# New ranks for a planned instruction order, one unit's sums moved to DMA, and a small copy moved to ScalarE

## The chip, the cores and the metric

The kernel runs on one core of a Trainium2 chip. The metric is the device time in microseconds; of several runs the median is taken. Lower is better.

## The reference, cut to what matters

Inputs are q, k, v and x of 2048 x 640 in bfloat16 (the reference passes q where the second block has its x), small filters, and weights of an MLP.

```python
# block A: a gated long convolution
k_shift = sum(k_pad[:, t:t + S, :] * shift_k[:, ks - 1 - t] for t in range(4))
kv = k_shift * v
y = irfft(rfft(kv, padded to 2S) * rfft(ssm_k, padded to 2S))[:S] + kv * ssm_D
a = q * y
# block B: a shifting MLP and a second MLP
h = gelu(layernorm(x) @ w1)
hs = concat(h quarters shifted by +1, -1, +2, -2 in the sequence) @ w2
x1 = x + hs
b = x1 + gelu(layernorm(x1) @ w3) @ w4
# both, gated
g = sigmoid((x * gate_w).sum(-1))
out = g * a + (1 - g) * b
```

## The kernel before

**One list, five queues.** The kernel does not write its instructions into the engines' queues directly. Each is put down as a node of a program `P` with its engine, what it reads and writes, an estimated cost and a tag; `P.stage` is appended to the tag, so that "mm1:2" is the first matmul of row group 2. `P.schedule` then makes the order: it keeps a clock of its own for TensorE, ScalarE, VectorE, GpSimd (POOL) and SyncE (SP), and picks again and again the node that can start earliest, and among equals the one of the highest rank. Ranks stand in the table `P.PRIO` by tag. The loads from HBM go through a model link of a given rate, so the clock also assumes when data arrives. The result is a fixed order for each engine; at run time each engine works through its queue in that order and waits on semaphores where needed. A node whose inputs come later on the chip than on the planner's clock holds up all that stands behind it in its queue.

**Storage.** All tiles lie in one SBUF tensor, "arena", so the profile calls nearly everything arena. PSUM is used as four pairs of banks.

**Block B.** Rows of x are laid out as 8 row groups (rho) of 2 x 128 partitions. Layer norm 1 takes its statistics by VectorE (`ln_bn`, bn_stats at L686, tags bn and ln) for rows 0 and 2 to 7, and by ScalarE sums (tags sum and sq, L496) for row 1. The reciprocal root is one POOL instruction (L661), then come a small product on VectorE (L662) and the normalised rows (L705, tag xn). TensorE transposes them (L718, tag xTp), ScalarE evicts them (xTe, by the helper at L511). `mm1` (L794) multiplies by w1: three jobs for each of four row pairs, the third with a small rearranged copy of w1, `w1t`, made by one copy of 128 x 640 (L565). The gelu evictions write HT. The shifts of the last quarter-columns are small POOL DMAs (L822, tag tail). Zeros at HT's edges are memsets (L779 for the pads, L784), and HT's first part holds the row of shift taps at the very start, so the pads wait for the four small matmuls that spread these taps over the partitions (L589, tag shk). The gate's sums are 80 one-column matmuls (L752). `mm2` (L840, and L843 for the residual) has four groups of four jobs, tags mm2:4 to mm2:7, then layer norm 2, `mm3` (L883, w3 in two halves; the second half lies where w2 was and is loaded after the last mm2) and `mm4` (L902), whose evictions are added to x by accumulating POOL DMAs (tag addB). mm3's results lie in 20 slots where HT was; one stage of mm3 fills 12.

**Block A.** VectorE forms k_shift * v (tags kv and kve, by the helper `tt` at L484; for the second half of the rows, two of the sums are accumulating POOL DMAs, kva). TensorE transposes the filter (L641, tag tap). Four units, one for each half of the channels and each half of the frequencies (0,0), (0,1), (1,0), (1,1), stages 0 to 3, are done as: forward transforms of filter and signal (L938, tags fwdh and fwdk), window and butterflies (win, bh, bk), a pointwise complex product (pw), and a fold. Units named in `PW_DMA` use `pointwise_dma`, which leaves two of the sums to accumulating POOL DMAs (L522, tags pwa with 320 KB and pwb with 640 KB); the others use `pointwise`, all on VectorE. After the units of a half, `inverse` (L1099) makes eight jobs; its evictions are scaled by the gate (gy), multiplied by q and added to x (fin; for half 0 the addition is a DMA, addy), and rows go out by SP.

**Loads.** All of x, w1, w2, k with its halo, v, the transform table FM and the filter (ssm) are loads on SP's queue without inputs, so their order is their rank. POOL loads w3, w4 and the table GM later.

Nodes of one tag share one rank in the kernel before:

```python
for n in self.nodes:
    n.prio = self.PRIO.get(n.tag, n.prio)
```

Of the kernel before, what the change touches and what calls it, by code (L numbers as in the profile page):

```python
# [10 lines left out]
ACTF = mybir.ActivationFunctionType  # L11
# [68 lines left out]
class Prog:  # L80
# [66 lines left out]

    def schedule(self):

        for n in self.nodes:  # L150
            n.base = frozenset(n.deps)
            for d in n.deps:
                d.users.append(n)
        for n in reversed(self.nodes):
            tail = max((u.prio for u in n.users), default=0.0)
            n.prio = tail + (n.cost if n.kind == "c" else n.cost + 2.0 + n.bytes / self.RATE)
        for n in self.nodes:
            n.prio = self.PRIO.get(n.tag, n.prio)
        self._forward()

    def _forward(self):
# [10 lines left out]
        known_at = {}  # L172
        pair_free = [0.0] * PAIRS
        pair_job = [None] * PAIRS
        link = 1.6
        xlink = 0.0

        def move(at, nbytes):
# [20 lines left out]
        while left:  # L199
# [16 lines left out]
            n = best[1]  # L216
            e = n.eng
# [6 lines left out]
            elif n.kind == "dma" and e == "pool" and n.bytes < self.SMALL:  # L224
                link = move(link, n.bytes)
                n.end = t + 4.5
            elif n.kind == "dma":
                link = move(max(link, t), n.bytes)
# [132 lines left out]
def bass_gated_mix__ssm_conv_h3__mixer_s_mlp__prompt_kernel(  # L361
# [9 lines left out]
    PW_NEG = ()  # L371
    BF_DMA = ()
    INV_SPLIT = ((1, 0), (1, 4))
    PW_DMA = ((0, 0), (0, 1), (1, 0))
    LN1_ROWS = ((0,), (1,), (2, 3), (4, 5), (6, 7))
    LN1_DVE, LN2_DVE = ((0,), (2, 3), (4, 5), (6, 7)), (0, 1)
    P = Prog(nc)
# [51 lines left out]
    w1t = V(oW12 + 3200, 640).rearrange("p (c f) -> p c f", c=5)  # L429
# [4 lines left out]
    GM = V(oGM, 4096).rearrange("p (a i r s k) -> p a i r s k", a=2, i=2, r=4, s=2)  # L434
# [9 lines left out]
    ident = V(oID, 128)  # L444
# [35 lines left out]
    def dve(fn, r, w, n, psum=False, tag="", **kw):  # L480
        return P.op("dve", lambda e, ps: fn(e), r=r, w=w, cost=c_dve(n, psum), tag=tag, **kw)
# [4 lines left out]
    def act(o, i, func, n, scale=None, bias=None, acc=None, tag="", group=None, job=None, accgroup=None):  # L486
        r = [x for x in (i, scale, bias) if x is not None and not isinstance(x, float)]
        kw = {}
        if scale is not None:
            kw["scale"] = scale  # L490
        if bias is not None:
            kw["bias"] = bias
        if acc is not None:
            kw["accum_out"] = acc
        naps = sum(1 for x in (scale, bias) if x is not None and not isinstance(x, float))
        node = P.op("act", lambda e, ps: e.activation(o, i, func, **kw), r=r, w=[o], cost=c_act(n, naps, acc is not None),  # L496
                    tag=tag, group=group)
        if acc is not None:
            P._track(node, [], [acc], accgroup)
        return node  # L500
# [58 lines left out]
    for c in range(2):  # L559
# [2 lines left out]
    load_halo(0)  # L562
    load_k(0, 0)
    w1s, w1d = w1v.rearrange("p c (g f) -> p c g f", g=4)[:, :, :, 128:160], w1t.rearrange("p c (g f) -> p c g f", g=4)
    P.op("pool", lambda e, ps: e.tensor_copy(w1d, w1s), r=[w1s], w=[w1d], cost=1.2, tag="w1t")  # L565
    load_k(0, 1)
    load_x("sp", 0, 4, 8)
    load_x("sp", 1, 4, 8)
# [3 lines left out]
          w=[GWT], nbytes=100000, after=[late], tag="gw")  # L572
# [184 lines left out]
    v0, r0, nm0 = [stat(0, f)[:, :, 0:2] for f in ("var", "rs", "nm")]  # L757
# [18 lines left out]
    SHIFT = [1, -1, 2, -2]  # L776
    for col in (0, 257):
        z = HT[:, 0:4, :, col:col + 1]
        dve(lambda e, z=z: e.memset(z, 0.0), [], [z], 32, group="pad")  # L779
    for j, d0 in enumerate(SHIFT):  # L780
        rs = slice(0, d0) if d0 > 0 else slice(8 + d0, 8)
        col = 1 if d0 > 0 else 256
        z = HT[32 * j:32 * j + 32, 4, rs, col:col + 1]
        dve(lambda e, z=z: e.memset(z, 0.0), [], [z], 2, group="tail")  # L784
    RAW = [V(oGM + 512 * i, 512) for i in range(2)]
    for sc in range(4):
        P.stage = sc
        for fp in range(3):
# [13 lines left out]
            else:  # L802
                raw = RAW[sc % 2]
                evict(job, raw, lambda ps: bank(ps, 0, 512), ACTF.Gelu_apprx_tanh, 512, tag="gelu1t")
                for j, d0 in enumerate(SHIFT):
# [4 lines left out]
                    for carry, lst in todo.items():  # L810
                        k0, rho0, n = lst[0][0], lst[0][1], len(lst)
# [8 lines left out]
                        else:  # L820
                            i = i.rearrange("p (r q) -> p r q", r=n)
# [265 lines left out]
    def inverse(half, slot0, slot1):  # L1087
# [50 lines left out]
    inverse(1, "s3", "k0")  # L1138

    P.PRIO = {  # L1140
# [25 lines left out]
    }  # L1166
    P.schedule()
    P.assign_waits()
# [30 lines left out]
```

## Time and profile before

| | us |
|---|---|
| median of 3 runs | 244.91 (243.86 to 245.47) |
| the profiled execution | 245.85 |
| its span | 244.1 |
| TensorE busy | 223.6 |
| VectorE busy | 215.7 |
| ScalarE busy | 154.3 |
| POOL busy | 57.9 |

The profile is of one execution. Its span runs from the first to the last instruction shown; the time has 1.75 us more around it. Busy times are sums of instruction lengths; issuing a DMA counts for none of the engines except where POOL makes it. In rows of the chain, a start and a length in us are followed by an engine or "issue" and a line of the kernel; in rows of the timeline, the number in brackets is the idle time before and what ended it.

### The profile page before, as it was taken

The page shows a single profiled execution, that of the slowest core. Times are in us where ns is not written, and L with a number is a line of the kernel's source. Part 1 is how long each engine was busy: PE and PEld are TensorE (multiplying, and loading weights), DVE is VectorE, ACT ScalarE, POOL GpSimd, SP SyncE. Part 2 cuts the span into 40 slices and gives each one's busy share as a digit, 9 for nine tenths or more (in the row PEclk, how much of TensorE's full clock was granted, in tenths as well). Part 3 has the DMA queues.
Part 4 walks back from the last instruction along what each step waited for, and adds up shares of the span by engine and source line. Part 5 has one row for each costly group of instructions (what it writes and reads, how often), then busy time and mean ns, then how long its engine had stood idle before and what let it go on. Part 6 is the DMA issues. An engine that isn't in the chain of part 4 may idle for free.

```text
span 244.1 us, 3961 instructions
## 1 busy us (share of the span) xinstructions
PE 223.6 (92%) x1557; PEld 142.4 (58%) x1569; DVE 215.7 (88%) x337; ACT 154.3 (63%) x236; POOL 57.9 (24%) x70
## 2 busy tenths in 40 slices
PE   0579999999999999969999999999999998999990
PEld 0236576577777775525677645577546773777760
DVE  4899989996999758998989699799994899999992
ACT  5536899647468999956997456652257224127881
POOL 5311452451013040145002121001220011015910
PEclk9999999979999999999999999999999999999997
DMA  6999998098019649665585325403248034934998
GB/s 217 369 398 331 397 362 301 22 246 156 3 19 191 88 113 293 141 129 107 106 104 183 56 51 77 85 3 54 53 56 110 0 55 70 382 88 74 160 214 253
DMA packets 29938, 37.32 MB, mean 153 GB/s; under 512 B 12464, under 2 KB 22960, under 8 KB 29792
## 3 DMA queue, kind: packets, MB, share of 16 engines
q0 software_dynamic: 9424, 15.21, 32.0%
q1 hardware_dynamic: 20496, 21.86, 29.7%
q8 instruction: 12, 0.20, 0.3%
q14 instruction: 6, 0.05, 0.1%
HBM read 21.79 MB, written 2.62 MB: 100 GB/s over the span
## 4 chain that ended last, share of the span: by engine, by line
PE 88%; DMA 5%; DVE 3%; ACT 1%; issue 1%; SPq 0%; ACTq 0%
PE PS L902 21%; PE PS L883 18%; PE PS L938 14%; PE PS L794 10%; PE PS L840 9%; PE PS L1099 7%; DMA arena<-in_B_w_dram 3%; PE PS L641 3%; PE PS L718 2%; PE PS L843 2%; DMA arena<-in_A_q_dram 1%; DVE arena L686 1%; ACT arena L511 1%; PE PS L752 1%; DVE arena L705 1%
## 5 line engine op out<-in xcount | busy, mean ns | idle before, releaser
L484 DVE TENSOR_TENSOR arena<-arena 128x1280 bf16<-128x1280 bf16 (+2 forms) x192 | 180.3, 999 | 12.3 <-ACT arena L511 9.9
L511 ACT ACTIVATE arena<-PS 128x640 bf16<-128x640 f32 (+3 forms) x129 | 96.6, 821 | 42.5 <-PE PS L883 21.9
L522 POOL DMA_DIRECT2D arena<-arena x26 | 29.4, 1207 | 106.3 <-ACT arena L511 64.8
L883 PE MATMUL PS<-arena 128*128 128x512 bf16 x232 | 51.9, 379 | 2.4 <-DMA arena<-in_B_w_dram 2.0
L902 PE MATMUL PS<-arena 128*128 128x320 bf16 x384 | 52.8, 299 | 1.1 <-ACT arena L511 1.1
L511 ACT ACTIVATE arena<-PS,arena 128x320 bf16<-128x320 f32 (+1 forms) x48 | 27.6, 615 | 36.9 <-PE PS L902 34.2
L902 PEld LDWEIGHTS PS<-arena 128*128 128x128 bf16 x384 | 37.5, 98 | 16.1 <-ACT arena L511 1.6
L883 PEld LDWEIGHTS PS<-arena 128*128 128x128 bf16 x240 | 23.3, 98 | 29.6 <-DMA arena<-in_B_w_dram 2.5
L938 PE MATMUL PS<-arena 128*128 128x320 bf16 x256 | 36.4, 299 | 0.0
L938 PEld LDWEIGHTS PS<-arena 128*128 128x128 bf16 x256 | 25.1, 98 | 10.6
L840 PE MATMUL PS<-arena 128*128 128x320 bf16 x160 | 27.6, 310 | 0.0
L794 PE MATMUL PS<-arena 128*128 128x512 bf16 x96 | 23.8, 404 | 1.6 <-ACT arena L511 1.4
L686 DVE BATCH_NORM_STATS2 arena<-arena 128x6 f32<-128x320 bf16 x44 | 19.0, 467 | 4.9 <-DMA arena<-in_A_q_dram 2.5
L496 ACT ACTIVATE arena<-arena 128x640 bf16<-128x640 bf16 (+2 forms) x30 | 21.8, 756 | 1.7 <-DMA arena<-in_A_q_dram 1.7
L840 PEld LDWEIGHTS PS<-arena 128*128 128x128 bf16 x160 | 16.1, 101 | 6.8
L794 PEld LDWEIGHTS PS<-arena 128*128 128x128 bf16 x100 | 10.0, 103 | 13.6 <-issue 4.4
L1099 PE MATMUL PS<-arena 128*128 128x320 bf16 x128 | 17.6, 299 | 0.0
L1099 PEld LDWEIGHTS PS<-arena 128*128 128x128 bf16 x128 | 12.5, 98 | 4.9
L661 POOL TENSOR_TENSOR arena<-arena 128x4 f32<-128x4 f32 (+1 forms) x9 | 10.1, 1118 | 16.7 <-DVE arena L691 11.4
L705 DVE TENSOR_SCALAR arena<-arena 128x640 bf16<-128x640 bf16 x32 | 12.4, 440 | 1.3 <-issue 1.2
L822 POOL DMA_DIRECT2D arena<-arena x18 | 9.7, 544 | 8.5 <-ACT arena L511 8.5
L645 ACT ACTIVATE arena<-PS 128x1280 bf16<-128x1280 bf16 x8 | 9.5, 1263 | 2.4 <-PE PS L641 2.4
(43 smaller groups left out, 73.3 us busy)
## 6 DMA issues: line engine op xcount, KB each, us to landing
arena<-arena POOLq DMA_DIRECT2D x7, 640.0 KB, 5.6
arena<-in_A_q_dram SPq DMA_DIRECT2D x6, 640.0 KB, 8.0
arena<-in_B_w_dram POOLq DMA_DIRECT2D x4, 960.0 KB, 7.7
arena<-arena POOLq DMA_DIRECT2D x11, 320.0 KB, 3.7
arena<-in_A_ssm_k_dram SPq DMA_DIRECT2D x5, 512.0 KB, 11.4
arena<-in_A_k_dram SPq DMA_DIRECT2D x4, 640.0 KB, 17.1
arena<-in_A_v_dram SPq DMA_DIRECT2D x4, 640.0 KB, 20.5
out_dram<-arena SPq DMA_DIRECT2D x16, 160.0 KB, 2.1
```

Of the source, the lines that this page charges most:

```text
L484: return dve(lambda e: e.tensor_tensor(o, a, b, op), [a, b], [o], n, tag=tag, **kw)
L496: node = P.op("act", lambda e, ps: e.activation(o, i, func, **kw), r=r, w=[o], cost=c_act(n, naps, acc is not None), tag=tag, group=group)
L511: node = P.op("act", lambda e, ps: e.activation(ov, inner(ps), func, **kw), r=r, w=[o], cost=c_act(n, len(r), acc is not None), job=job, t ...
L522: P.dma("pool", lambda e, ps: e.dma_start(o, i, accum_op=ALU.add, max_dma_last_dim=2560), r=[o, i], w=[o], nbytes=3 * 256 * n, cost=1.2, t ...
L686: dve(lambda e, o=o, x=x: e.bn_stats(o, x), [x], [o], 640, tag="bn", group=("bn", l, rho, c))
L705: P.op("dve", lambda e, ps, b=b, x=x, rs=rs, nb=nb: e.tensor_scalar(b, x, rs, nb, op0=ALU.mult, op1=ALU.add), r=[x, rs, nb], w=[b], cost=0 ...
L794: fns.append(lambda e, ps, b=b, c=c, lhsT=lhsT, sc=sc: e.matmul(bank(ps, b, 512), lhsT, XT[:, c, 2 * sc:2 * sc + 2, :], start=(c == 0), st ...
L840: fns.append(lambda e, ps, hh=hh, ft=ft, lhsT=lhsT, last=by_dma and ft == 4: e.matmul(bank(ps, hh, 320), lhsT, w2v[:, ft, 320 * hh:320 * h ...
L883: fns.append(lambda e, ps, b=b, ft=ft, c=c, sc=sc: e.matmul(bank(ps, b, 512), w3v[ft // 6][:, c, 128 * (ft % 6):128 * (ft % 6) + 128], XT[ ...
L902: fns.append(lambda e, ps, hh=hh, ft=ft, lhsT=lhsT: e.matmul(bank(ps, hh, 320), lhsT, w4v[:, ft, 320 * hh:320 * hh + 320], start=(ft == 0) ...
L938: fns.append(lambda e, ps, r=r, ri=ri, s=s, b=b, rhs=rhs: e.matmul(bank(ps, b, 320), FM[:, kap, r, s, ri, :], rhs, start=(s == 0), stop=(s ...
L1099: fns.append(lambda e, ps, kap=kap, ri=ri, c=c, r=r, s=s: e.matmul(bank(ps, c, 320), GM[:, kap, ri, r, s, :], Qs[kap][:, r, ri, c, :], sta ...
```

## The change

- `PW_DMA` gets (1, 1), so the last unit, too, leaves two sums to POOL DMAs.
- w1's small copy moves from POOL to ScalarE.
- The pads get a tag of their own, with ranks.
- In the planner's clock the link starts at 0.8 in place of 1.6.
- Nodes of one tag are split into up to four parts, in their order of writing, with a rank each: "mm1:2.0" is the first quarter of mm1's stage 2. All ranks are new. Where a tag has one node only, it keeps its name.

```diff
-        for n in self.nodes:
-            n.prio = self.PRIO.get(n.tag, n.prio)
+        parts = {}
+        for n in self.nodes:
+            parts.setdefault(n.tag, []).append(n)
+        for tag, ns in parts.items():
+            for i, n in enumerate(ns):
+                if len(ns) > 1:
+                    n.tag = f"{tag}.{i * min(len(ns), 4) // len(ns)}"
+                n.prio = self.PRIO.get(n.tag, self.PRIO.get(tag, n.prio))
...
-        link = 1.6
+        link = 0.8
...
-    PW_DMA = ((0, 0), (0, 1), (1, 0))
+    PW_DMA = ((0, 0), (0, 1), (1, 0), (1, 1))
...
-    P.op("pool", lambda e, ps: e.tensor_copy(w1d, w1s), r=[w1s], w=[w1d], cost=1.2, tag="w1t")
+    act(w1d, w1s, ACTF.Copy, 640, tag="w1t")
...
-        dve(lambda e, z=z: e.memset(z, 0.0), [], [z], 32, group="pad")
+        dve(lambda e, z=z: e.memset(z, 0.0), [], [z], 32, group="pad", tag="pad")
...
-        dve(lambda e, z=z: e.memset(z, 0.0), [], [z], 2, group="tail")
+        dve(lambda e, z=z: e.memset(z, 0.0), [], [z], 2, group="tail", tag="pad")
```

Ranks that the prediction speaks of, before and after (quarters 0 to 3 where there are several):

```
                 before   after
shk (the load)   151      247
x0, x1, x2       180 186 158   217, 212, 186 183
w1               147      182
x4               126      178
w2               96       119 146 95 39
k1               26       47 148
ln:0             103      140 60 235 74
bn:2             11       228 144 101 248
xn:0, xn:1       33, 97   230 198, 50 86
mm1:0            77       64 57 59
mm1:2            47       113 295 201
mm2:5            32       190 271 217 259
mm2:6            10       195 156 184 249
mm2:7            104      183 159 190 158
gate             54       181 179 68 97
tap:1            114      154 291 248 136
fwdh:1           59       223 219 160 12
fwdk:1           25       148 206 213 241
fwdk:2           86       45 124 288 103
mm4:2            30       21 11 4 32
addB:3           3        207 193
pwb:3            (none)   22
```

112 rows, old and new, of the table final are left out of this document.

## The prediction

> **What bounds the kernel now.** First the page's busy times and its slices, then the chain of work that ended last, in order of time, then what each engine did around the places where that chain is not matmuls.
>
> ```profile
> span 244.1 us, 3961 instructions
> PE 223.6 (92%) x1557; PEld 142.4 (58%) x1569; DVE 215.7 (88%) x337; ACT 154.3 (63%) x236; POOL 57.9 (24%) x70
> PE   0579999999999999969999999999999998999990
> DVE  4899989996999758998989699799994899999992
> PEclk9999999979999999999999999999999999999997
> ```
>
> TensorE is full from the third slice to the last but one; VectorE is nearly as full. Both matter: whoever moves one must keep the other fed. The chain, with its few places that are not plain matmul time:
>
> ```profile
> 9.78 0.15 DVE arena L705
> 12.41 1.24 PE PS L718 x10
> 13.67 1.25 ACT arena L511
> 15.05 6.45 PE PS L794 x20
> ...
> 50.41 1.33 PE PS L840 x5
> ...
> 58.64 0.68 PE PS L840 x5
> ...
> 99.94 8.15 DMA arena<-in_B_w_dram
> 108.14 5.79 PE PS L883 x26
> ...
> 220.15 17.40 PE PS L1099 x128
> ```
>
> Columns are start, length, what. Dense TensorE work begins at 15.05 (mm1, L794) and ends at 220.15 + 17.40 = 237.55; 6.6 us of last eviction, products and output follow. In these 222.5 us TensorE is short of four things. Two are idle time: 2.03 us before 108.14, while the second half of w3 arrives, and 1.11 us at 206.94 (mm4 of the last stage behind a gelu eviction). Two are slow matmuls: the first 20 of L794 take 6.45 us where 19 later ones take 4.26 (about 2.0 us lost), and after the gate's one-column matmuls five L840 take 1.33 instead of 0.68, twice, and one L843 0.27 instead of 0.14: 1.4 us lost. The rest of the time can only go by another start, another end, or new holes.
>
> The w3 hole, and the start of the kernel on VectorE and GpSimd (start, length, engine):
>
> ```profile
> 99.47 6.64 PE L883 MATMUL PS<-arena 128*128 128x512 bf16 x29
> 108.14 6.65 PE L883 MATMUL PS<-arena 128*128 128x512 bf16 x29 [2.03 <-DMA arena<-in_B_w_dram]
> ```
>
> ```profile
> 9.84 0.22 DVE L779 MEMSET arena<- 128x32 bf16 x2
> 10.13 0.43 DVE L705 TENSOR_SCALAR arena<-arena 128x640 bf16<-128x640 bf16 x1
> 10.42 0.72 POOL L565 COPY arena<-arena 128x640 bf16<-128x640 bf16 x1 [1.61 <-DMA arena<-in_B_w_dram]
> 10.49 0.67 DVE L662 TENSOR_TENSOR arena<-arena 128x2 f32<-128x2 f32 x1
> ```
>
> The load of w3's second half is issued at 99.94, when the last mm2 matmul (L843) has ended, and takes 8.15 us; 29 mm3 matmuls cover 6.64 of them. At the start, the pads and a small product stretched beside GpSimd's copy (0.67 us; the nine L662 have a median of 0.16) lie between row 0's and row 1's normalised halves, which the first transposes await.
>
> **The change, part by part.** All sums are against the profiled execution's own 245.85 us (span 244.1 and 1.75 around it); the median of the three runs is 244.91, 0.94 below, and the same difference is then taken from it.
>
> *Pads and w1's copy.* The two memsets cost 0.15 of VectorE time on the chain (9.98 to 10.13 less the issue), the copy some 0.5 (0.67 less 0.16). The copy becomes one 640-element ScalarE activation: 0.75 us by the row of L496 (792 ns mean). ScalarE sits idle 1.49 us before the first transposes' eviction and 4.47 before the first gelu, so it costs nothing; without that cover, 0.75.
>
> *Shift taps' row first.* One more SP issue of 0.33 us lies ahead of x0. Its matmuls (2.42 us from 7.24) and four evictions (2.49 us from 8.00) go some 4 us earlier, into time in which TensorE and ScalarE mostly idle; but on ScalarE they now stand ahead of row 1's four sums (3.93 to 6.92 before), which then end near 8.6.
>
> *Ranks, at the start.* With the new table row 0's mean sign (ln:0.1, 60) and its normalise wait behind statistics of rows 2 and 3 (bn:2, 101 to 248), and row 1's normalise has 50 and 86. From the end of row 0's statistics (6.85) I lay out eight statistics of 0.41 and four aggregates of 0.12, 3.8 us; four normalised halves, 1.6; small products 0.8; pads 0.15: row 1 is ready at 13.2 instead of 12.27, +0.9. In return rows 2 and 3 are ready early: 20 transposes (1.12 us at 21.50) move into idle time before mm1, and take part of its slow stretch, half of 1.1, with them: -1.1 -0.5. If the 1.14 us that VectorE stood with nothing shown before 9.78 are not repeated, it is earlier by that; if they come on top, later. Start and slow stretch together: -0.7 by these rows; I take -0.5, ends -1.8 and +2.0.
>
> *Ranks, in the middle.* All mm2 jobs now have 156 or more, above much of the forward transforms (fwdh:1.3 has 12, fwdk:1.0 148, fwdk:2.0 45); before, mm2:6 had 10 and came last. mm2 is 16 jobs of 1.63 us, 26.1; from 50.41, with three forward transforms of 4.35 between, it ends near 50.4 + 26.1 + 13.1 + 1.4 = 91, not 99.65. The w3 load then lands near 100, and behind mm2 there are 6.6 us of mm3 on the first half and at least one transform of 4.35, together more than 8.15. So the 2.03 us go: -2.0, ends 0 and -2.0. It rests on the load not standing in POOL's in-order queue behind an accumulate that waits for VectorE. The hole of 1.11 at 206.94 stays: mm3's last jobs reuse activation slots that mm4:2 reads, and mm4:2 has the lowest ranks (4 to 32), so the same order closes the stage. Ends 0 and -1.1, value 0.
>
> *Ranks, the gate.* gate.0 is at 181, above the last transposes of the taps (tap:1.0 154, tap:1.3 136); before, gate and taps lay back to back for 3.1 us (47.30 to 50.41), and the clock fell. If only the gate's 2.3 us lie together the 1.4 us may partly go. Value -0.5, ends 0 and -1.4.
>
> *Last unit's sums.* Two VectorE sums go: one of 1280 (0.82) and one of 2560 (1.49), 2.3 us. Two accumulates come on POOL's queue, 1.2 us each to issue, 3.7 us (320 KB) and 5.6 us (640 KB) to land. After the larger is issued VectorE still has 1.49 + 0.82 + 1.49 + 0.82 of products and 1.6 of folds that don't read its result, 6.2 against about 5.6 to 6.8: covered. The fold's last operations ended near 233, where the inverse's fifth job of half 1 (220.15 + 8.7 + 4.35 = 233.2) needs them. So the 2.3 us bring nothing to TensorE by themselves, but let its end come up to 2.3 us earlier without waiting. Value 0, ends 0 and +5 (below).
>
> *Queue order of the loads.* The same bytes, other order: w2's last quarter (39) and k's third block (47) are last, where w2 was issued at 4.78. Value 0, ends 0 and +3.
>
> Sum: -0.5 -2.0 -0.5 = -3.0: 242.85 for a run like the profiled one, **241.9** for the median.
>
> **The rivals.**
> *Gains spent again (about 244.9).* The start comes +2.0 and the w3 hole closes by as much: 0. For it: VectorE is 88% busy and its list is served in a fixed order, so an early hole closed is a later one opened (it already stood 3.67 us before the last unit). Against it: TensorE has 50 us of mm4 to fill with.
> *Loads late (247.4), the other side.* TensorE's queue is in order. Before, the loads ended with the seventh slice (301 GB/s, then 22), about 43 us, and mm1 ended at 47.3. mm2:5 has 217 to 271 in three of its quarters, above mm1:2.0 (113) and mm1:0 (57 to 64), so mm2 may stand near 40 in the queue; w2's last quarter then holds everything behind it for 3 us, and VectorE's third shift unit waits for k as long. 244.9 + 3.0 less the 0.5 of the start. It decides once mm2 stands ahead of about 43 us. Against it: mm2 also needs all of mm1 for most rows.
> *The last sum behind POOL's queue (about 247).* POOL waited 11.27 us for the addB at 214.76 and 5.67 for the one at 221.28. If the large accumulate (rank 22, addB:3 193 and 207) stands behind the second, it lands near 228, eight folds of 0.75 follow, and the inverse waits about 5 us: 241.9 + 5.
> *The slow matmuls.* The rows show slow matmuls after time with little TensorE work, and none later. If the 1.4 us after the gate go wholly: 241.9 - 0.9 = 241.0; if a further such stretch comes, 243.3. The Trainium skill (TensorE: Matmul & The Clock Gate, "The HAM clock gate") says that the clock is halved by default and released after some 3.4 us of sustained work, in windows that run freely. The trace agrees in the granted clock of 0.50 from 50 to 53 us; by that rule alone the place of the gate among the mm1 jobs settles this rival.
>
> **How the numbers follow.** Forecast 0.42 (own range 240.2 to 243.8); gains spent again 0.20; loads late 0.18; last sum late 0.08; slow matmuls otherwise 0.12. About 1%, 2.45 us, is what a measurement of this kernel can tell from no change. Faster by more: two thirds of the forecast, most of the last rival, a little of the second: 0.44. Slower by more: the two late cases and a part of the spent one: 0.26. Within: 0.30. The range runs from 238.6 (start -1.8, w3 -2.0, gate -1.4, and the 1.1 hole) to 248.0 (loads late, above).
>
> **What would show it.** Right: the first L794 between 14.5 and 16, transposes of rows 2 and 3 before it; no DMA piece of in_B_w_dram in the chain and the last L843 before 93; VectorE's last fold at or before 231; the first L1099 near 217. Wrong: TensorE idle near 40 to 45 with a load as its releaser, L1099 waiting for L484, an L522 behind ScalarE in front of the last folds, or VectorE idle for more than the 16 us that its waits from 59 to 223 us add up to now.

## The result, and the profile after

| | before | after |
|---|---|---|
| median, us | 244.38 (243.79 to 245.47) | 246.91 (246.15 to 247.69) |
| the profiled execution | 245.85 | 246.95 |
| its span | 244.1 | 245.2 |
| TensorE busy / VectorE busy | 223.6 / 215.7 | 223.4 / 214.1 |

The ratio after to before is 1.0142, 95% interval 1.0095 to 1.0188, from four runs of each: the change makes the kernel 1.4% slower, where 1.2% faster was forecast (241.9 to 244.91). All lines behind the planner's stand 7 lines further down in the kernel after (mm1 is L801, mm2 L847 and L850, mm3 L890, mm4 L909, the forward transforms L945, the inverse L1106, VectorE's `tt` L491, the eviction helper L518, POOL's accumulates L529, loads L525, the DMA transposes L719).

The page of after, busy times and slices (share of the span in brackets; tenths in forty slices):

```profile
span 245.2 us, 3981 instructions
PE 223.4 (91%) x1569; PEld 141.9 (58%) x1569; DVE 214.1 (87%) x335; ACT 155.6 (63%) x237; POOL 62.1 (25%) x71
PE   3099999899999999959999999999999998999990
DVE  4979999799995979989949999999994999973992
PEclk9999999999999999979999999999999999999999
```

TensorE's row is as full as before but for the ends and one dip; the granted clock falls in the 18th slice, near 107 us; the drop of the clock near 50 us, in the ninth slice of before, is gone. TensorE's timeline in after, from the first transposes on, only rows with idle time in front of them (start, length, line, shapes, count, idle time and its releaser):

```profile
12.55 4.00 PE L725 MATMUL PS<-arena 128*128 128x128 bf16 x40 [7.54 <-DVE arena L698]
48.08 1.26 PE L945 MATMUL PS<-arena 128*128 128x320 bf16 x8 [0.73 <-DVE arena L771]
51.13 0.84 PE L847 MATMUL PS<-arena 128*128 128x320 bf16 x5 [0.16 <-ACT arena L652]
107.67 6.11 PE L890 MATMUL PS<-arena 128*128 128x512 bf16 x20 [3.03 <-DMA arena<-arena]
208.09 13.21 PE L909 MATMUL PS<-arena 128*128 128x320 bf16 x96 [1.12 <-ACT arena L518]
```

At its first mm3 matmul, 93.68, all mm2 and 128 transform matmuls are done. Before has done as much, and 20 mm3 matmuls (4.32 us) besides, at 99.65, so its equal mark is 95.33: after is 1.65 ahead. At the first mm4 it is behind, 125.52 to 124.39, with equal work done (100 mm3 and 168 transform matmuls against 90 and 184, 10 x 0.216 for 16 x 0.136). So 2.8 us go between the two marks, although before has its own hole of 2.03 there. The chain of waits shows the place (start, length, what):

```profile
95.94 0.37 DVE arena L712
96.31 0.02 issue
96.33 11.09 DMA arena<-arena
107.42 0.25 issue
107.67 6.11 PE PS L890 x20
...
221.31 7.61 PE PS L1106 x56
...
228.93 9.97 PE PS L1106 x72
```

Layer norm 2 of a row group is done at 96.31, its DMA transpose (tag xT) is issued at 96.33 and lands 11.09 us later. (The inverse then begins at 221.3, not near 217, and TensorE ends at 238.9 instead of 237.55.) What stands ahead of it is on POOL's timeline, and what is usual for a transpose in the answer for L719 (us to landing, least, median, most):

```profile
93.48 2.64 POOL L525 DMA_DIRECT2D arena<-in_B_w_dram  x3 [4.25 <-DMA arena<-arena]
```

```profile
DMA to landing us min/median/max: 2.6/2.7/11.1
```

Three loads of 960 KB, w3's second half and both halves of w4, go out in one 2.64 us piece just before the transpose. In before the longest landing of a transpose was 6.3, and the same loads lay far apart:

```profile
87.72 1.75 POOL L518 DMA_DIRECT2D arena<-in_B_w_dram  x2 [8.46 <-DMA arena<-arena]
99.94 0.92 POOL L518 DMA_DIRECT2D arena<-in_B_w_dram  x1 [9.41 <-PE PS L843]
```

The kernel makes all three wait for the DMA transposes of rows 0 and 1 (`after=turned[4]`), w3's half also for the last mm2. In before, w4's two left when these transposes had landed, at 87.72, and w3's half 12 us later, behind mm2. In after the transposes land later, at 93.48, and mm2 has ended by then (near 91); w3's half is first in POOL's queue, w4's two are next, and all three leave together. The windows of after then show the second price, the granted clock behind the hole (window, its length, PE busy, and further on PEclk, DMA share, GB/s):

```profile
100.00:107.00 7.00, 4.63 (x22) 1.96 (x20) 7.00 (x10) 6.65 (x13) 1.39 (x2) 1.00 1.20 263
107.00:109.00 2.00, 1.33 (x4) 0.53 (x5) 2.00 (x3) 0.00 (x0) 2.00 (x2) 0.65 0.97 140
109.00:111.00 2.00, 2.00 (x6) 0.63 (x5) 1.06 (x4) 0.00 (x0) 1.65 (x2) 0.50 1.07 193
111.00:113.60 2.60, 2.60 (x13) 1.18 (x12) 2.57 (x7) 1.94 (x2) 1.01 (x1) 1.00 0.77 144
```

The 20 matmuls take 6.11 us instead of the 4.32 of the next such group in the chain: 1.8 lost on top of 3.03 (together 4.8).

The start (VectorE, ScalarE) answers the lines shown of before:

```profile
6.62 0.09 DVE L786 MEMSET arena<- 128x32 bf16 x1
11.61 0.80 DVE L712 TENSOR_SCALAR arena<-arena 128x640 bf16<-128x640 bf16 x2
12.39 0.80 DVE L712 TENSOR_SCALAR arena<-arena 128x640 bf16<-128x640 bf16 x2
11.34 0.74 ACT L503 ACTIVATE arena<-arena 128x640 bf16<-128x640 bf16 x1 [2.08 <-DMA arena<-in_B_w_dram]
```

The pads come early and the copy fits into ScalarE's idle time, but both pairs of normalised halves come late, since statistics and sums of other rows are ahead of them.

### The profile page after: what moved, and what is told of

Its sections match the earlier page's. It is cut to its first block, busy times and chain, and to the rows that moved or that the text cites. A ratio compares the mean times of both kernels' runs of the same rounds, so it can differ in the third digit from the quotient of the medians.

```text
span 245.2 us, 3981 instructions
## 1 busy us (share of the span) xinstructions
PE 223.4 (91%) x1569; PEld 141.9 (58%) x1569; DVE 214.1 (87%) x335; ACT 155.6 (63%) x237; POOL 62.1 (25%) x71
## 4 chain that ended last, share of the span: by engine, by line
PE 68%; DMA 11%; SPq 11%; DVE 4%; ACT 2%; issue 1%; ACTq 0%; DVEq 0%
PE PS L909 21%; PE PS L890 17%; SPq L525 11%; PE PS L945 11%; PE PS L847 8%; PE PS L1106 7%; DMA arena<-in_A_k_dram 7%; DMA arena<-arena 5%; DVE arena L491 3%; ACT arena L518 2%; PE PS L801 2%; PE PS L850 2%; ACT arena L652 0%; PE PS L648 0%; DVE arena L712 0%
## 5 line engine op out<-in xcount | busy, mean ns | idle before, releaser
L491 DVE TENSOR_TENSOR arena<-arena 128x1280 bf16<-128x1280 bf16 (+2 forms) x190 | 178.1, 994 | 16.2 <-ACT arena L518 9.8
L518 ACT ACTIVATE arena<-PS 128x640 bf16<-128x640 f32 (+3 forms) x129 | 97.7, 814 | 40.4 <-PE PS L890 21.9
L529 POOL DMA_DIRECT2D arena<-arena x28 | 32.4, 1256 | 115.2 <-ACT arena L518 73.1
L890 PE MATMUL PS<-arena 128*128 128x512 bf16 x240 | 54.7, 387 | 3.0 <-DMA arena<-arena 3.0
L909 PE MATMUL PS<-arena 128*128 128x320 bf16 x384 | 53.5, 299 | 1.1 <-ACT arena L518 1.1
L518 ACT ACTIVATE arena<-PS,arena 128x320 bf16<-128x320 f32 (+1 forms) x48 | 27.4, 619 | 38.2 <-PE PS L909 35.1
L909 PEld LDWEIGHTS PS<-arena 128*128 128x128 bf16 x384 | 37.5, 98 | 16.4 <-ACT arena L518 1.6
L890 PEld LDWEIGHTS PS<-arena 128*128 128x128 bf16 x240 | 23.8, 99 | 31.7 <-issue 5.7
L945 PE MATMUL PS<-arena 128*128 128x320 bf16 x256 | 38.0, 299 | 0.7 <-DVE arena L771 0.7
L945 PEld LDWEIGHTS PS<-arena 128*128 128x128 bf16 x256 | 24.8, 98 | 11.4 <-DVE arena L771 0.9
L847 PE MATMUL PS<-arena 128*128 128x320 bf16 x160 | 26.3, 299 | 0.2 <-ACT arena L652 0.2
L503 ACT ACTIVATE arena<-arena 128x640 bf16<-128x640 bf16 (+2 forms) x31 | 22.5, 749 | 4.8 <-DVE arena L773 2.2
L801 PE MATMUL PS<-arena 128*128 128x512 bf16 x100 | 22.9, 379 | 0.0
L847 PEld LDWEIGHTS PS<-arena 128*128 128x128 bf16 x160 | 15.6, 98 | 6.6 <-issue 0.5
L1106 PE MATMUL PS<-arena 128*128 128x320 bf16 x128 | 17.7, 299 | 0.0
L668 POOL TENSOR_TENSOR arena<-arena 128x4 f32<-128x4 f32 (+1 forms) x9 | 12.0, 1335 | 20.2 <-DVE arena L698 14.0
L801 PEld LDWEIGHTS PS<-arena 128*128 128x128 bf16 x100 | 9.6, 98 | 10.3
L1106 PEld LDWEIGHTS PS<-arena 128*128 128x128 bf16 x128 | 12.4, 98 | 5.1 <-ACT arena L518 0.3
L712 DVE TENSOR_SCALAR arena<-arena 128x640 bf16<-128x640 bf16 x32 | 13.1, 439 | 1.0 <-PE PS L725 0.8
L725 PE MATMUL PS<-arena 128*128 128x128 bf16 x80 | 6.8, 250 | 7.7 <-DVE arena L698 7.5
L829 POOL DMA_DIRECT2D arena<-arena x18 | 9.6, 542 | 11.5 <-ACT arena L518 11.4
```

The lines of the kernel that those rows point to most:

```text
L491: return dve(lambda e: e.tensor_tensor(o, a, b, op), [a, b], [o], n, tag=tag, **kw)
L518: node = P.op("act", lambda e, ps: e.activation(ov, inner(ps), func, **kw), r=r, w=[o], cost=c_act(n, len(r), acc is not None), job=job, t ...
L529: P.dma("pool", lambda e, ps: e.dma_start(o, i, accum_op=ALU.add, max_dma_last_dim=2560), r=[o, i], w=[o], nbytes=3 * 256 * n, cost=1.2, t ...
L801: fns.append(lambda e, ps, b=b, c=c, lhsT=lhsT, sc=sc: e.matmul(bank(ps, b, 512), lhsT, XT[:, c, 2 * sc:2 * sc + 2, :], start=(c == 0), st ...
L847: fns.append(lambda e, ps, hh=hh, ft=ft, lhsT=lhsT, last=by_dma and ft == 4: e.matmul(bank(ps, hh, 320), lhsT, w2v[:, ft, 320 * hh:320 * h ...
L890: fns.append(lambda e, ps, b=b, ft=ft, c=c, sc=sc: e.matmul(bank(ps, b, 512), w3v[ft // 6][:, c, 128 * (ft % 6):128 * (ft % 6) + 128], XT[ ...
```

## The experiments

In each, the ratio is to runs of before made beside it on the same chip. Where a DMA is moved, one line puts a named instruction of one queue before or behind another of the same queue; nothing else of the order changes.

### Two runs at the suspects alone, and both together

**Both w4 loads moved back** behind the first unit's pwa accumulate, in POOL's queue of after:

```diff
+    shift_node("pool", "w4.0", 0, "after", "pwa:0")
+    shift_node("pool", "w4.1", 0, "after", "pwa:0")
```

> The changed kernel with one move in POOL's queue: the two loads of w4 are issued after the first unit's small accumulate instead of right behind w3's second half; every other queue keeps its order. Theory A (three loads of 960 KB, issued together at 93.5 to 96, stand in front of the last transpose of rows 2 and 3, which takes 11.1 us to land; TensorE then stands 3.0 us and runs 20 matmuls in 6.1 instead of 4.3 us): the transpose lands in under 7 us, the hole of 3.0 before mm3 of rows 2 and 3 and the slow stretch of 1.8 go, time 246.9 - 4.8 = 242.1. Rival B (the hole is that of w3's second half, as in the kernel before, or the transposes are late in any case, because their rows are normalised late): w4's place does nothing, 246.9 within 0.5. Rival C (the wait moves on): mm4 or the first unit's VectorE sums wait for w4 or for accumulates beside it, 245 to 247.

Measured: 244.32 us, ratio 1.0072 (1.0036 to 1.0109), against 1.0142: 0.7% back. TensorE's timeline, rows near the old hole:

```profile
121.32 1.31 PE L945 MATMUL PS<-arena 128*128 128x320 bf16 x8 [1.08 <-ACT arena L518]
123.63 6.68 PE L909 MATMUL PS<-arena 128*128 128x320 bf16 x48 [1.00 <-ACT arena L518]
```

The hole and the half clock are gone (68 mm3 matmuls run through, 15.06 us from 94.36), so the loads made both. The two intervals still overlap a little; that the time falls is firmer in the two runs below that move more. Of the 4.8 us, 2.1 come back as two waits for ScalarE's evictions a few us later. The chain of this run shows what ScalarE waited for:

```profile
107.39 12.21 DMA arena<-arena
...
119.70 0.84 DVE arena L491
120.56 1.30 ACT arena L518 x2
```

The DMA is the first unit's 640 KB accumulate (tag pwb). It is now issued right behind the two moved loads (POOL issues them from 103.84 to 106.09) and takes 12.21 us to land, where it took 5.7 in after. VectorE stands 3.65 us for it, and ScalarE 2.98 us for VectorE. So these two waits are a price of the place to which the experiment moved the loads, as its rival C said, and not of the new ranks. The wait for k near 48 us is also longer here than in after, 1.43 us for 0.73.

**The second unit's k earlier** on SP's queue of after:

```diff
+    shift_node("sp", "k1.0", 0, "before", "v1.0")
```

> The changed kernel with one move in SP's queue: the third block of k is loaded three places earlier, before v's last two blocks. Theory A (VectorE's 1.45 us wait for k at 45 delays the gate's products, and with them TensorE by 0.7 and 0.2 us near 48 and 51): these waits go, the hole near 104 stays, time 246.9 - 0.9 = 246.0. Rival (VectorE's wait is regained later and TensorE's small holes come from elsewhere): 246.9 within 0.3.

Measured: 245.82, ratio 1.0107 (1.0061 to 1.0152). The holes at 48 and 51 us are gone; the one before mm3 stays, and is no smaller for coming earlier:

```profile
106.14 5.53 PE L890 MATMUL PS<-arena 128*128 128x512 bf16 x19 [3.19 <-DMA arena<-arena]
```

The gain of 0.35% is not clear of noise by itself: the two intervals overlap widely. It fits the trace of after, where the chain has k's DMA for 16.47 us up to 44.95 and VectorE idle for 1.45 us for it at 45.04.

**Both moves together.**

> Both moves together, w4's loads back and k's third block earlier. If the two waits are separate, their gains add: 246.9 - 4.8 - 0.9 = 241.2. If the hole before mm3 is only put off by TensorE's being earlier (its rows come by VectorE's time, not TensorE's), the second gain is lost: 242.1.

Measured: 244.09, ratio 1.0047 (1.0012 to 1.0082). The two gains add (0.7 and 0.35 of a percent make 1.05; 0.95 measured), and the waits for ScalarE (1.11 and 1.00) stay, with the 640 KB accumulate again 12.2 us in flight. The interval lies wholly below that of after, so the two moves together are clear of noise. 0.5% of loss is left.

### The price of the half clock by itself

14 matmuls of 128x512 whose results nobody reads, put in TensorE's queue of after in front of the mm3 job that waits for the transpose; the hole stays a hole, but the array works in it.

```diff
...
+    P.fill, P.fill_after, P.fill_count = fill, [last], 14
+    P.fill_fn = lambda e, ps: e.matmul(bank(ps, 0, 512), ident, V(oFM, 512), start=True, stop=True)
```

> The changed kernel with 14 matmuls of 128x512 that nobody reads put into TensorE's queue just ahead of the mm3 job that waits for the transposes of rows 2 and 3; they take 14 x 0.216 = 3.0 us of the hole. Theory A (idle time in TensorE costs a second time, by the half granted clock after it): the hole is filled, the 20 matmuls behind it take 4.3 instead of 6.1 us, time 246.9 - 1.8 = 245.1. Rival (the slow matmuls come from something else than the idle time, such as the weight loads beside the arriving w3): 6.1 stays, 246.9 or a little over.

Measured: 244.75, ratio 1.0097 (1.0056 to 1.0138).

```profile
106.03 2.97 PE L1249 MATMUL PS<-arena 128*128 128x512 bf16 x13
108.84 4.48 PE L897 MATMUL PS<-arena 128*128 128x512 bf16 x20
```

L1249 are the idle matmuls, L897 the 20 that took 6.11 us. They take 4.48 now. The whole kernel gains 0.45% by the medians, somewhat less than the 1.6 us (0.7%) that the row shows, again with intervals that overlap.

### The last unit's sums

**On VectorE again**, in the order of after. The planner runs anew on the edited list: up to the last unit the order stays, but the inverse's jobs, their evictions and the output rows change places too, which the expectation did not count on.

```diff
-    PW_DMA = ((0, 0), (0, 1), (1, 0), (1, 1))
+    PW_DMA = ((0, 0), (0, 1), (1, 0))
```

> The changed kernel with the last unit's two sums given back to VectorE (PW_DMA without (1, 1)); TensorE's, ScalarE's and SP's orders stay as they are. Theory A (the loss comes from the ranks; TensorE sets the end and VectorE has slack in the last unit: it stood 4.55 us near 223): the same time as the changed kernel, ratio to before 1.014 within 0.004. Rival (the two accumulates stand in POOL's queue and hold the last folds up): ratio falls by 0.01 or more. Other rival (VectorE's 2.3 us were needed): ratio rises by up to 0.01.

Measured: 245.86, ratio 1.0106 (1.0057 to 1.0155): 0.36% less than after. TensorE ends at the same time (238.87 in after, 238.93 here) with no wait in the inverse in either. The two intervals overlap widely. The difference that the traces show lies behind TensorE's end, on SP. SP's rows for output rows, and what its waits were, first of after, then of this run:

```profile
L1133 SPq DMA_DIRECT2D out_dram<-arena x16: 372/496/507, 230.2 to 242.6; - x16
SPq L1133 <- DVE arena L491: 4.5, 1, 4.5
```

```profile
L1133 SPq DMA_DIRECT2D out_dram<-arena x16: 372/494/573, 230.4 to 241.8; - x16
SPq L1133 <- DVE arena L491: 3.1, 2, 2.7
```

After's first four rows go out at the same time, but the fifth waits 4.5 us for its product and starts at 236.78 instead of 235.62; from there SP issues one row each 0.53 us, back to back, to the end. The span ends 6.3 us behind the last matmul instead of 5.9. Whether the sums or the new places of the rows make SP wait is not told apart.

**The sums by DMA in the order of before**, as the only edit (the planner again changes the places of the inverse's jobs, nothing ahead of the last unit):

```diff
-    PW_DMA = ((0, 0), (0, 1), (1, 0))
+    PW_DMA = ((0, 0), (0, 1), (1, 0), (1, 1))
```

> The kernel before with one part alone: the last unit's two sums by DMA. TensorE's, ScalarE's and SP's orders do not change, VectorE's changes in the last unit only. Theory A (the added accumulates move 1.9 MB through the DMA engines beside the last addB, and the inverse's evictions wait for addB to have read their buffers, 2.7 us in the run with all small parts): TensorE stands 1 to 1.5 us at the fourth or fifth inverse job, ratio 1.003 to 1.006. Rival (the sums cost nothing, and the loss with all small parts came from the start): 1.000 within 0.003. Other rival (VectorE's 2.3 us help): 0.995.

Measured: 244.41 to 243.75, ratio 1.0036 (0.9999 to 1.0074). Here the price lies on TensorE. Its timeline, and ScalarE's:

```profile
225.93 9.95 PE L1099 MATMUL PS<-arena 128*128 128x320 bf16 x72 [1.05 <-ACT arena L511]
224.93 1.78 ACT L511 ACTIVATE arena<-PS,arena 128x320 bf16<-128x320 f32 x4 [2.27 <-DMA arena<-arena]
```

The inverse's evictions stand still for 2.27 us for a DMA: they write the buffers that the last mm4 results' addB reads, and that accumulate, issued behind the pwb of 640 KB that is now in flight with it, takes 6.5 us to land instead of 3.7. Both runs put the price near 0.4%, where I had 0; neither is clear of noise by itself.

### The small parts with the ranks of before

Before with the sums by DMA, w1's copy on ScalarE, the pads' tag and shk and pad at rank 188, all other ranks as before and whole tags (the planner orders anew, so this is not before's order with four edits):

```diff
-    PW_DMA = ((0, 0), (0, 1), (1, 0))
+    PW_DMA = ((0, 0), (0, 1), (1, 0), (1, 1))
...
-    P.op("pool", lambda e, ps: e.tensor_copy(w1d, w1s), r=[w1s], w=[w1d], cost=1.2, tag="w1t")
+    act(w1d, w1s, ACTF.Copy, 640, tag="w1t")
...
-        dve(lambda e, z=z: e.memset(z, 0.0), [], [z], 32, group="pad")
+        dve(lambda e, z=z: e.memset(z, 0.0), [], [z], 32, group="pad", tag="pad")
-        dve(lambda e, z=z: e.memset(z, 0.0), [], [z], 2, group="tail")
+        dve(lambda e, z=z: e.memset(z, 0.0), [], [z], 2, group="tail", tag="pad")
-        ... "shk": 151, ...
+        ... "shk": 188, "pad": 188, ...
```

> The kernel before with the three small parts alone: the last unit's sums by DMA, w1's copy on ScalarE, pads with a tag and the shift taps' load ahead of x (both of rank 188); the old ranks of whole stages and the old start of the link's clock. Theory A (the ranks bring the loss): the start is up to 1 us earlier, the rest like the kernel before, ratio 0.995 to 1.003. Rival (the small parts themselves cost, or any new plan falls by as much): ratio 1.005 or more.

Measured: 246.1, ratio 1.0113 (1.0061 to 1.0165). It has the same wait in the inverse, longer:

```profile
228.60 9.95 PE L1099 MATMUL PS<-arena 128*128 128x320 bf16 x72 [1.48 <-ACT arena L511]
```

Beside it TensorE has four small holes of 0.26 to 0.51 (1.5 in all) and begins mm1 at 15.82. It says that a loss of this size can come without the new ranks; it can't say more, because the new order came with its own holes.

### How firm is the profile of before?

Before, profiled anew twice, one execution each:

> The kernel before, unchanged, profiled a second time: its first profiled execution (245.85) is above nearly all its runs (median 243.1). Theory A: the 1.4 us of slow matmuls after the gate, or some of the 2.0 us of slow matmuls at the start of mm1, do not come in every execution; this one shows less of them and 242 to 244 us. Rival: the same slow stretches, and other holes differ, such as that before w3's second half.

> The kernel before, unchanged, profiled a third time. Theory A (the hole of 2.03 us before w3's second half depends on the execution: it was there in the first profile and not in the second, in which the load had the same issue but TensorE came later by slow matmuls): with a start like the second's there is no hole; the time is 241 to 245. Rival: the hole is there as a rule, and the second profile was the exception.

Measured: 244.27 (span 242.5) and 241.96 (span 240.2), beside the first one's 245.85 (244.1). TensorE's timeline behind mm2 in the third execution:

```profile
97.48 13.11 PE L883 MATMUL PS<-arena 128*128 128x512 bf16 x58
```

and the chain behind the gate in the second, then the third:

```profile
51.68 1.33 PE PS L840 x5
```

```profile
50.68 0.68 PE PS L840 x5
```

| feature of before | first | second | third |
|---|---|---|---|
| w3's second half, issue to landing | 8.2 | 5.7 | 5.8 |
| w3 hole | 2.03 | none | none |
| first 20 mm1 matmuls | 6.45 | 7.30 | 6.14 |
| lost behind the gate | 1.4 | some 1.7 | none |
| mean granted clock | 0.987 | 0.985 | 0.993 |

The 2.03 us hole on which most of the forecast rested is a feature of one execution; the three runs that keep before's order in the middle (idle matmuls, sums by DMA, taps first) have none, none and 0.16 us there, with the same load landing in 5.9 to 6.3 us. The clock behind the gate changes from one execution to the next, and it is worth most: over the 92 repeats of before in these comparisons, 56 have a mean granted clock of 0.983 to 0.988 and the other 36 one of 0.989 to 0.998. In each of the four series the median of the first group is 243.7 to 244.1 and that of the second 241.9 to 242.0. The mean also counts a drop behind the last matmul (in the third execution the only one, 0.50 from 238 us on), so near 0.990 it doesn't tell whether the gate's drop was there.

**After, profiled anew:**

> The changed kernel, unchanged, profiled a second time. Theory A: the hole of 3 us for the transposes of rows 2 and 3 and the slow matmuls behind it come again, at 246 to 247 us. Rival: the hole depends on the execution, and is under 1 us here.

Measured: 245.98 (span 244.2). The hole is there again, and the half clock behind it:

```profile
106.64 6.16 PE L890 MATMUL PS<-arena 128*128 128x512 bf16 x20 [2.75 <-DMA arena<-arena]
```

Five profiles that have the three loads in one piece show it (3.03, 2.75, 3.19, 2.96, and filled in the fourth experiment): it belongs to the order, not to the execution. In equal work against before's second profile, after's is 2.70 ahead at the first mm3 (92.93 to 95.63) and 1.89 behind at the first mm4 (124.55 to 122.66): 4.6 lost, the hole and the clock.

### The start

**Shift taps first on SP's queue of before**, alone:

```diff
+    shift_node("sp", "shk", 0, "before", "x1")
```

> The kernel before with one part alone: the load of the shift taps is moved from the fifth place of SP's queue to the first; nothing else moves. Theory A (x's loads come 0.4 us later and the start hangs on them; the taps' matmuls run early, and in TensorE's idle time): mm1 begins 0.3 to 0.6 us later, ratio 1.001 to 1.003. Rival (the taps' four evictions stood in the way of the first transposes' on ScalarE): mm1 begins earlier by up to 0.5, ratio 0.998.

Measured: 243.41, ratio 0.9989 (0.9955 to 1.0023): no difference. The tap matmuls come 5 us earlier (2.32 for 7.24), the first mm1 at 14.30 instead of 14.64 to 15.05, and its first 20 matmuls still take 6.88.

**Idle matmuls in TensorE's empty start of before**: two of 128x512 before the transposes of xTp:0, one before those of xTp:1, three before the first mm1; nobody reads them.

```diff
...
+    warm("xTp:0", 0, 2)
+    warm("xTp:1", 0, 1)
+    warm("mm1:0", 0, 3)
```

> The kernel before with six matmuls of 128x512 that nobody reads put into TensorE's idle time at the start: two before the first ten transposes, one before the second ten, three before the first mm1. All queues keep their order. Theory A (TensorE's first four to five us of dense work run at half speed, 2.1 to 3.0 us lost in mm1 in the two profiles of before, and the changed kernel has that behind it by the time mm1 begins, because 40 transposes stand in a row before it): the first 20 mm1 matmuls take 4.3 to 5.4 us instead of 6.5 to 7.3, ratio 0.990 to 0.996. Rival (mm1 is slow because of its weights or the loads that arrive beside it): no change, 1.000 within 0.003, or slower by what the fill delays the transposes (up to 0.5 us).

Measured: 241.85 to 243.75, ratio 0.9936 (0.9903 to 0.9968): faster than both kernels. TensorE's timeline (L804 is mm1 here, with the numbers 10 lines further down than in before):

```profile
15.51 4.48 PE L804 MATMUL PS<-arena 128*128 128x512 bf16 x19 [0.70 <-ACT arena L521]
```

mm1 starts 0.5 to 0.9 us later, and its first matmuls take 4.48 for what took 6.14 to 7.30. (The granted clock reads 1.00 from 12 to 24 us in before as well, so the slow start shows in the matmuls' lengths alone.) This execution has the drop behind the gate, 0.56 and 0.59 from 48 to 52 us, and takes 242.68; the two profiles of before's order that have this drop and no large hole, the second one of before and that of the taps, take 244.27 and 243.85. So 1.2 to 1.6 us are gained in like with like; whether a different share of repeats with the drop is also in the 0.64% stays open. Of the change's own gain at the start (after's 30 mm1 matmuls take 6.64) this is the part that can be had without moving anything.

### All three undone

After with both w4 loads moved back, k earlier and the last unit's sums on VectorE; ranks by quarters, pads, taps and copy stay.

```diff
-    PW_DMA = ((0, 0), (0, 1), (1, 0), (1, 1))
+    PW_DMA = ((0, 0), (0, 1), (1, 0))
+    shift_node("pool", "w4.0", 0, "after", "pwa:0")
+    shift_node("pool", "w4.1", 0, "after", "pwa:0")
+    shift_node("sp", "k1.0", 0, "before", "v1.0")
```

> The kernel after with three edits undone together: both w4 loads moved behind pwa:0 on POOL's queue, the second unit's k before its v on SP's, and the last unit's sums (1,1) on VectorE again instead of by DMA. What stays of the change: shift taps and ranks as they are in after, pads and w1's copy off VectorE's way. Theory (three separate causes that add): 1.0142 less 0.0095 (both loads, after to e3) less 0.0036 (sums, after to e5) gives about 1.001, within 1% of before on either side of nothing; the trace shows no hole over 0.3 us with a DMA releaser before the third product, no 1.4 us wait of the last inverse for L518 with an addB DMA behind it, and no wait for k at 45. Rival (the sums' price was only the shift of the last unit against a late stage, and is gone where the stage is not late): as e3_both, 1.005. Second rival (the new order of ranks costs by itself, through ScalarE's evictions in 97 to 120): 1.005 or more, with holes of 1 us or more ahead of the last mm3 and first mm4, released by ScalarE, as in e3_both, and these alone make up what is left.

Measured: 243.11 to 243.25, ratio 1.0007 (0.997 to 1.0044). The three together make up the whole loss, and the interval lies wholly below that of after. Holes of dense work on TensorE, all that are over 0.3 us:

```profile
120.14 1.31 PE L945 MATMUL PS<-arena 128*128 128x320 bf16 x8 [0.55 <-ACT arena L518]
122.45 6.68 PE L909 MATMUL PS<-arena 128*128 128x320 bf16 x48 [1.00 <-ACT arena L518]
205.02 13.21 PE L909 MATMUL PS<-arena 128*128 128x320 bf16 x96 [1.12 <-ACT arena L518]
```

What is left of the change is even with before as a whole, not free. Its profile has no clock drop behind the gate (mean 0.998; the 12 repeats have 0.990 to 0.998), and yet it has the median of 243.11 between before's repeats with the drop (243.8 in this series) and without it (241.9). Beside before's third profile, which has no drop either, the trace gives that difference of 1.2: mm1 begins at 17.18, 2.2 us later, with 1.1 us more of transposes done; the two ScalarE waits of 1.55 are new, and are again the price of w4's new place (the 640 KB accumulate takes 11.7 us to land, VectorE stands 3.1 for it); and the first mm1 matmuls lose 0.4 (28 in 6.42) where before's lose 1.8 (20 in 6.14). 2.2 - 1.1 + 1.55 - 1.4 is 1.25. No run moves w4's loads to a place where they are in nobody's way, so what the rest of the change is worth without these waits stays open.

## Why the prediction was wrong, point by point

**"Ranks, in the middle": -2.0, measured a loss, 2.8 us between the two marks and 0.7% of the time by the experiment.** This step failed twice. Its size came from the hole of one execution, which two further profiles don't have, so that for most runs there was nothing to gain. And its reasoning stopped at w3's load. mm2 did end early, as worked out (last L850 near 91, forecast 91), and no in_B_w_dram piece is in the chain. But the new order also put w4's two loads directly behind w3's, and the transposes of rows 0 and 1, for which all three wait, landed 5.8 us later than before and behind mm2's end; so three loads of 960 KB left together ahead of the transpose that mm3's next job needs. I had weighed the POOL queue for an accumulate in front of the load, and not the loads in front of SP's transposes. The price in the trace is 2.75 to 3.19 of hole and 1.8 of half clock; the one experiment gets only 0.7% of the time back, since its place for w4's loads costs 2.1 us anew.

**"Ranks, the gate": -0.5, ends 0 and -1.4.** The stretch went wholly, as in the rival "The slow matmuls". Its size, 1.4 to 1.7 when it comes, is absent in part of before's executions anyway. That rival's other half came true as well, at a place it didn't name: a new slow stretch, behind the new hole. The Trainium skill (TensorE: Matmul & The Clock Gate, "The HAM clock gate") has the array at half clock by default and released after some 3.4 us of work, in free-running windows. The granted 0.50 at 109 to 111 us and the changes from execution to execution agree. Its summary of the idle side, a window of some 3.4 us, is longer than the hole of 2.75 us that was already enough here; the 2.03 us of before were not.

**The start: -0.5, ends -1.8 and +2.0.** mm1's slow stretch went, as said and by more (30 matmuls in 6.64); but the first L801 came at 16.38, outside the 14.5 to 16 given, because statistics and sums of other rows pushed the normalised halves to 11.6 and 12.4. That is 1.33 later with 1.12 us of transposes more behind it, 0.2 lost, and 2.1 us of slow matmuls saved: -1.9, at the lower end given. By the first mm3, 1.65 are left, though the gate's 1.4 came to it and only 0.9 of new holes went from it; some 0.75 of this I can't place.

**"Last unit's sums": 0, ends 0 and +5.** Measured +0.4% in two pairs of runs, neither clear of noise by itself. The rival "The last sum behind POOL's queue" had the right resource, and not the path: the inverse doesn't wait for folds, but evictions wait for the addB (before's order), or the output rows begin late (after's). The 2.3 us saved on VectorE became idle time: it waits 4.55 us for ScalarE before 223.57. The trace accounts for about half of the price in after's order.

**"Loads late" (0.18).** Right that k's third block would come late, VectorE waiting at 45 us and TensorE behind it; wrong in size, 0.73 and 0.16 us of holes, 0.35% by the experiment, instead of 3.0; no mm2 stood waiting for w2.

**What held.** w1's copy on ScalarE (0.74 us in 2.08 of idle time) cost nothing that the trace shows, the taps neither gave nor took, and the wait of 1.1 before the last mm4 stayed, as written.

**The rival that was missing:** several large transfers that wait for one event leave at once, and a small one that is needed first is behind them. "Gains spent again" came nearest in spirit, but has neither the place nor the sign.

## What to carry to other kernels

When a new order moves a stage, list what each large DMA near it waits for, which of them will now leave together, and which smaller transfer is issued behind them. The same question goes to every repair: here the moved loads stood in front of an accumulate instead of a transpose. Before a hole of 2 us goes into a forecast, a second profile should have it. And a hole of some 3 us on TensorE had two prices here, the idle time and the slow matmuls after it, of which the second can be bought back with matmuls that nobody reads.

## What the runs showed of the hardware

- A DMA transpose that lands in 2.7 us by the median took 11.1 behind three 960 KB loads from another engine's queue. A 640 KB accumulate that lands in 5.7 us in after took 11.7 to 12.2 behind two such loads. The Trainium skill (DMA: Bandwidth & Descriptors, "Issuing engines are not separate DMA queues") says that DMAs of all issuing engines run on the same 16 DMA engines; the trace fits this, with a DMA share of 1.20 and 263 GB/s from 100 to 107 us.
- A load of the same bytes at the same place took 8.2, 5.7 and 5.8 us in three executions of one kernel. Why the first took longer stays open.
- Holes of 2.75 to 3.19 us were followed by a granted clock of 0.50 to 0.70 for some 3 us. In part of before's executions so was the gate, 80 one-column matmuls that the profile shows as busy without a gap.
- Six idle matmuls in an empty start went with a time 0.64% lower here (0.32 to 0.97), with the first 20 mm1 matmuls in 4.48 us instead of 6.14 to 7.30.
